# Eighty loads instead of eighty-eight: joining transfers in a two-layer decode kernel that reads its whole cache

## The chip, the cores and the metric

The kernel runs on one NeuronCore of a Trainium2 chip. The time is that of the device, in microseconds, for one execution; less is better. Beside plain runs there is one execution under the hardware profiler, and all rows below are from it.

## The reference, cut to what matters

Two layers, each used twice in turn: attention over a cached window for one new token of 4 sequences, with 32 heads, and a small MLP. The window is the last 1024 positions.

```python
x = x + A(layernorm(x));  x = x + B(layernorm(x));  x = x + A(layernorm(x));  x = x + B(layernorm(x))
def A(x):                       # B=4, D=640, 32 heads of 128, W=1024 cached positions
    q = x @ wq                                  # wq 640 x 4096
    p = softmax(einsum(q, k_cache[-W:]) * Dh**-0.5)
    return einsum(p, v_cache[-W:]) @ wo         # wo 4096 x 640
def B(x):
    return relu(x @ w1) @ w2                    # w1 640 x 1728, w2 1728 x 640
```

All of it is float32. Both rounds use the same caches and weights, and on-chip memory holds about a sixth of them, so nearly everything is read twice from HBM.

## The kernel before, in words

**Records.** For each head the host lays out one record of 9472 columns on 128 partitions (`REC`): columns 0 to 640 are wq (`WQ`), 640 to 4736 the keys (from `K`), 4736 to 8832 the values (from `V`), 8832 to 9472 wo (from `WO`). `VH` is 2048, half of the keys or the values. One column over 128 partitions is 512 bytes, so a record is 4,736 KB and 640 columns are 320 KB. `wm` holds w1 (five blocks of 1728 columns) and w2 (54 tiles of 160).

**Rounds.** `order` gives the heads: 0 to 31 in round one; in round two the five heads still on chip, 27 to 31, come first, then 0 to 26. `store` holds five whole records and 2,176 columns more; `home` says in which of its five slots a head lies. A small tile `kept` holds the end of head 26, and `ring` takes MLP weights and some pieces.

**Loads.** All loads stand in one list, `items`, in a fixed order, and all are issued by SyncE. `pump` issues the next one as soon as the columns that it overwrites are no longer in `live`; `done` and `free` take columns out of `live` after the last instruction that reads them. `pump` is called while the program is built, so on the chip this becomes a wait of the load for that instruction. `group` loads five records in three transfers (`FIVE`), `LAST_FIVE` in four. `ending` cuts the last three heads of a round (a, b and c) into keys and values. In round one `ending` also loads, last of all, the wo of the last six heads (`late`), 26 to 31. The list `places` fills the places that come free at the start of round two.

**Eight semaphores.** Transfers signal their landing on eight semaphores in turn (`DMAHW0` to `DMAHW7`). A transfer that is issued while the one eight places before it is still under way waits until that one has landed. So the moment of such an issue tells when the transfer eight places before it landed.

**Compute.** For each head `query` projects q, `scores` multiplies with the keys in two halves, `softmax` and `weights` run on VectorE and ScalarE, `values` multiplies with the values in two halves, `picks` and `output_T` gather the head's output, and `project` multiplies with wo into `acc`. In the loop the order on TensorE is: scores of head n+1, values of head n, query of head n+2, output and projection of head n. `center` and `deviation` are the layer norm, `mlp` the MLP, `busy` fills TensorE with matmuls that nobody reads.

**Parking.** At the end of round one the MLP needs room, so `park` copies 2560 columns of head 31 from `store` to PSUM, and `unpark` copies them back, into head 27's slot, at the start of round two.

Every instruction is issued through one helper, so nearly all rows carry its line, L102.

Of the kernel before, what the change touches and what calls it, by code (L numbers as in the profile page):

```python
# [39 lines left out]
B, D, H, DH, W, FF = 4, 640, 32, 128, 1024, 1728  # L40
# [6 lines left out]
WQ, K, V, WO = 0, D, D + 4 * W, D + 8 * W  # L47
REC = 2 * D + 8 * W
HALF = REC // 2
VH = 2 * W  # L50

NS = 5
# [7 lines left out]
KEPT = WO - 4 * 512  # L60
FIRST = K + 3 * 512
# [12 lines left out]
IN_RING = [(2176, 4736, "spare", 0), (4736, 6272, "ring", 0), (6272, 8832, "ring", 1536)]  # L74

CUTS = [*range(0, K, DH), *range(K, WO, 512), *range(WO, REC + 1, FD)]
W1_SLOT = [[0, 1], [2, 3], [4]]
W2_SLOT = [22, 20, 8, 4]
LATE = 6


FIVE = [REC + 6272, 2 * REC - 3072, 2 * REC - 3200]
LAST_FIVE = [REC + 4736, 2 * REC - 4736, REC, REC]
THREE = [REC + HALF, REC + HALF]
GROUPS = [{h: FIVE for h in range(0, 25, 5)}, {6: THREE, 9: FIVE, 14: FIVE, 19: LAST_FIVE}]


class InOrder:
# [21 lines left out]
def decode_kernel(ctx: ExitStack, tc: tile.TileContext, xf, rec, wm, out):  # L110
    nc = tc.nc
    pe, dve, act, pool, sp = (InOrder(tc, e) for e in (nc.tensor, nc.vector, nc.scalar, nc.gpsimd, nc.sync))
# [23 lines left out]
    store = sb.tile([P, FIRST + NS * REC], F32, name="store")  # L136
    kept = sb.tile([P, REC - KEPT], F32, name="kept")
# [39 lines left out]
    LAST = H - NS  # L177


    def home(h, r):  # L180

        if r:
            return FIRST + (h if h >= LAST else h - 6 + LAST) % NS * REC
        return (0 if h < NS else FIRST) + h % NS * REC

    items = []

    at = {("rec", 1, LAST - 1): [(KEPT, REC, "kept", 0)], ("rec", 1, 0): [(0, FIRST, "store", 0)]}
    live = []
    spare = home(H - 1, 0)  # L190
    buffers = {"store": store, "ring": ring, "kept": kept}

    def load(src, lo, hi, buf, col, parts):
        items.append((src[:, lo:hi], buf, col, hi - lo, parts))

    def place(buf, col):
        return ("store", spare + FROM + col) if buf == "spare" else (buf, col)
# [1 line left out]
    def weight(r, lo, hi, buf, col):  # L199
        buf, col = place(buf, col)  # L200
        load(wm, lo, hi, buf, col, [(("w", r), lo, hi, col)])


    def run(r, lo, hi, buf, col):
        parts = [(("rec", r, h), max(lo - h * REC, 0), min(hi - h * REC, REC), col + max(h * REC - lo, 0))
                 for h in range(lo // REC, (hi - 1) // REC + 1)]
        load(rec, lo, hi, buf, col, parts)

    def piece(r, h, lo, hi, buf="store", col=None):
        run(r, h * REC + lo, h * REC + hi, buf, home(h, r) + lo if col is None else col)  # L210


    def group(r, h, sizes):
        lo = 0
        for size in sizes:
            run(r, h * REC + lo, h * REC + lo + size, "store", home(h, r) + lo)
            lo += size

    def ending(r, hs, late):
        a, b, c = hs[-3:]  # L220
        end = WO if late else REC
        for h, lo, hi in ((a, 0, V), (b, 0, V), (a, V, end), (c, 0, V), (b, V, end), (c, V, WO if late else KEPT)):
            piece(r, h, lo, hi)
        if late:
            for h in hs[-1:] + hs[-LATE:-1]:
                if h == LAST - 1:
                    piece(r, h, WO, REC, "kept", WO - KEPT)
                else:
                    piece(r, h, WO, REC)


    hs = order[0]
    for h in hs[:-3]:
        if h in GROUPS[0]:
            group(0, h, GROUPS[0][h])
        if h >= 25:
            piece(0, h, 0, KEPT if h == LAST - 1 else WO if h >= H - LATE else REC)
        if h == LAST - 1:
            piece(0, h, KEPT, WO, "kept", 0)
    ending(0, hs, True)  # L240
    for lo, hi, buf, col in MLP_RING:
        weight(0, lo, hi, buf, col)


    hs = order[1]
# [4 lines left out]
    for lo, hi, buf, col in IN_RING:  # L250
        piece(1, new[0], lo, hi, *place(buf, col))
    places = [("store", old[i] + lo, old[j] + hi) for i, lo, j, hi in (
        (0, 0, 0, K), (0, K + 1024, 0, K + VH), (0, K + VH + 1536, 0, V), (1, 0, 1, K), (1, K, 1, K + VH), (1, K + VH, 1, V),
        (0, V, 0, WO), (2, 0, 2, V), (1, V, 1, REC), (3, 0, 3, V), (2, V, 2, REC), (3, V, 4, FROM))]
    places += [("store", 0, FIRST), ("store", old[4] + FROM, old[4] + REC), ("ring", 0, RING)]
    cuts = [h * REC + x for h in new[1:6] for x in CUTS]
    c, end = new[1] * REC, new[6] * REC
    for buf, lo, hi in places:
        if lo == old[1]:
            piece(1, new[0], WO, REC, buf, lo)  # L260
        elif c < end:
            cut = max(x for x in cuts if x <= min(end, c + hi - lo))
            run(1, c, cut, buf, lo)
            c = cut
    assert c == end
    for h in new[6:-3]:
        if h in GROUPS[1]:
            group(1, h, GROUPS[1][h])
        if not any(g <= h < g + sum(z) // REC for g, z in GROUPS[1].items()):
            piece(1, h, 0, REC)  # L270
    ending(1, hs, False)
    for ks in W1_SLOT:
        weight(1, ks[0] * FF, (ks[-1] + 1) * FF, "store", home(LAST + 1, 0) + ks[0] * FF)
    n = 0
# [4 lines left out]
    def pump():  # L279

        while items:
            src, buf, col, n, parts = items[0]
            if any(b == buf and x < col + n and col < y for b, x, y in live):
                return
            sp.dma_start(buffers[buf][:, col:col + n], src)
            live.append((buf, col, col + n))
            for key, lo, hi, c in parts:
                at.setdefault(key, []).append((lo, hi, buf, c))
            items.pop(0)

    def pieces(key):
# [9 lines left out]
    def done(key, lo, hi):  # L301

        if key[0] == "rec" and key[1] == 0 and key[2] >= LAST:
            return
        if key == ("rec", 0, 0):
            lo = max(lo, FIRST)
        for x, y, buf, col in pieces(key):
            free(buf, col + max(lo, x) - x, col + min(hi, y) - x)
        pump()
# [12 lines left out]
    def park(i):  # L322
        a = spare + FROM
        to, lo, hi = ((misc, 0, 512), (t_ps, 512, 1024), (sc_ps[1], 1024, 2048), (o_ps, 2048, 2560))[i]
        act.copy(to, store[:, a + lo:a + hi])
        free("store", a + lo, a + hi)
        pump()

    def unpark(i):
        b = home(LAST, 0)  # L330
        a = b + (K, K + 512, K + VH, K + VH + 512, K + VH + 1024)[i]
        copy = dve.tensor_copy if i in (0, 2) else act.copy
        copy(store[:, a:a + 512], (sc_ps[1][:, :512], sc_ps[1][:, 512:], o_ps, misc, t_ps)[i])
        live.append(("store", a, a + 512))
        if i == 2:
            dve.memset(o_ps, 0.0)
        if i == 4:
            c = spare
            at["rec", 1, H - 1] = [(0, FROM, "store", c), (FROM, V, "store", a - 512), (V, V + 1024, "store", b + K),
                                   (V + 1024, V + 1536, "store", b + K + VH), (V + 1536, REC, "store", c + V + 1536)]  # L340


    h_ps, warm = sc_ps[0][:, :512], sc_ps[0][:, 512:]
# [152 lines left out]


    pump()
    pe.matmul(acc[:, :FD], to_blocks, x_rows, start=True, stop=False, skip_group_check=True)
    for r in range(2):  # L500
        hs = order[r]
        late = LATE if r == 0 else 2
# [6 lines left out]
        if r:  # L509
            unpark(2)  # L510
            unpark(3)
        weights(0, ((0, 1), (1, 2)))
        for n, h in enumerate(hs[:-2]):
            i = n - (H - late)
# [5 lines left out]
            end = n == H - 3  # L520
# [82 lines left out]
```

## Time and profile before

| | |
|---|---|
| time, median of 3 runs | 711.78 us (711.56 to 711.82) |
| the profiled execution's own time | 712.25 us |
| its span, first to last instruction | 710.5 us |
| bytes read from HBM | 301.34 MB, 424 GB/s over the span |
| busy share of TensorE, VectorE, ScalarE | 72%, 41%, 14% |
| mean granted TensorE clock | 0.803 |

A span has 1.7 us around it in this execution (712.25 less 710.5). The rows are of the span, in microseconds from its start.

### The profile page before, as it was taken

To read this page: it belongs to the slowest core of one execution; us is meant where nothing else is said; L and a number is where in the kernel's file an instruction comes from. 1 tells how busy PE (TensorE), PEld (TensorE's weight loads), DVE (VectorE), ACT (ScalarE), POOL (GpSimd) and SP (SyncE) were. 2 spreads that over 40 slices of the span, in tenths; PEclk is the share of its full clock that TensorE was granted. 3 is DMA by queue.
4 is the path that set the end of the run, shared out by engine and by line. 5 is a ranking of instruction groups with operands and counts; after the bars stand their busy time and mean duration, and the time that the engine had idled before them with its cause. 6 is when DMAs were issued, how large, how long until landed. Compare 5 with 4: busy or idle time off the path is not lost.

```text
span 710.5 us, 8480 instructions
## 1 busy us (share of the span) xinstructions
PE 513.0 (72%) x3722; PEld 214.0 (30%) x3722; DVE 293.3 (41%) x518; ACT 99.7 (14%) x210; POOL 1.1 (0%) x9
## 2 busy tenths in 40 slices
PE   0777586677584578869888999656584678686986
PEld 0332232232331223333323443222241232332322
DVE  3242353243342343435531775525162243453651
ACT  0110110011010110111120422101010011011110
POOL 0000000000000000000000000000000000000000
PEclk9977787677778776877999999968597677777989
DMA  9999999999999999999999999999999999999996
GB/s 398 439 416 447 425 435 443 414 439 450 418 435 441 424 437 421 423 439 423 430 398 403 412 426 433 445 435 437 431 435 426 438 436 430 432 432 416 433 425 281
DMA packets 12596, 301.96 MB, mean 425 GB/s; under 512 B 1408, under 2 KB 1552, under 8 KB 4624
## 3 DMA queue, kind: packets, MB, share of 16 engines
q1 hardware_dynamic: 12528, 301.42, 98.9%
q8 instruction: 29, 0.48, 0.2%
q14 instruction: 7, 0.06, 0.0%
q10 hardware_dynamic: 32, 0.01, 0.0%
HBM read 301.34 MB, written 0.08 MB: 424 GB/s over the span
## 4 chain that ended last, share of the span: by engine, by line
DMA 72%; PE 23%; DVE 4%; issue 1%; ACT 1%; ACTq 0%; SPq 0%; DVEq 0%
DMA store<-rec 65%; PE sc_ps L102 9%; PE o_ps L102 6%; DMA store<-wm 4%; PE acc L102 3%; PE misc L102 3%; DMA ring<-wm 2%; DVE scratch L102 2%; PE t_ps L102 1%; DVE o_ps L102 1%; ACT oTs L102 1%; DVE small L102 0%; DVE sc_ps L102 0%; ACT sc_ps L102 0%; ACTq L102 0%
## 5 line engine op out<-in xcount | busy, mean ns | idle before, releaser
L102 PE MATMUL sc_ps<-store,qT 128*32 128x512 f32 x1024 | 194.5, 849 | 35.7 <-DMA store<-rec 34.3
L102 PE MATMUL misc<-xT,store 128*128 128x4 f32 x620 | 95.6, 281 | 109.8 <-DMA store<-rec 109.8
L102 DVE TENSOR_REDUCE small<-sc_ps 128x1 f32<-128x1024 f32 x64 | 78.4, 1224 | 181.3 <-PE sc_ps L102 181.2
L102 PE MATMUL o_ps<-store,scratch 128*16 128x512 f32 x960 | 149.5, 701 | 1.7 <-DMA store<-rec 1.4
L102 PEld LDWEIGHTS misc<-xT,store 128*128 128x128 f32 x620 | 90.2, 227 | 166.6 <-DMA store<-rec 119.4
L102 ACT ACTIVATE sc_ps<-sc_ps,small 128x1024 f32<-128x1024 f32 x64 | 69.8, 1091 | 322.6 <-DVE small L102 322.6
L102 DVE STREAM_TRANSPOSE sc_ps<-sc_ps 128x1024 f32<-128x1024 f32 (+1 forms) x70 | 80.8, 1155 | 0.1
L102 PEld LDWEIGHTS sc_ps<-store,qT 128*32 128x32 f32 x1024 | 41.5, 139 | 112.4 <-issue 60.7
L102 PEld LDWEIGHTS o_ps<-store,scratch 128*16 128x16 f32 x960 | 33.8, 117 | 117.4 <-issue 107.8
L102 DVE TENSOR_TENSOR o_ps<-o_ps,of_block 128x512 f32<-128x512 f32 x62 | 43.3, 699 | 50.6 <-PE o_ps L102 50.6
L102 DVE TENSOR_TENSOR qT<-misc,rows 128x4 f32<-128x4 f32 x61 | 9.5, 155 | 112.9 <-PE misc L102 112.9
L102 PE MATMUL acc<-store,oTs 128*4 128x160 f32 x488 | 34.1, 363 | 17.0 <-ACT oTs L102 17.0
L102 DVE TENSOR_REDUCE scratch<-o_ps 128x128 f32<-128x512 f32 x62 | 42.9, 691 | 2.1
L102 ACT COPY oTs<-t_ps 128x4 f32<-128x4 f32 x59 | 9.6, 163 | 207.4 <-PE t_ps L102 207.4
L102 PE MATMUL t_ps<-rows,scratch 128*128 128x4 f32 x118 | 25.8, 289 | 11.3 <-DVE scratch L102 10.3
L102 PEld LDWEIGHTS t_ps<-rows,scratch 128*128 128x128 f32 x118 | 21.9, 231 | 17.4 <-DVE scratch L102 13.1
L102 DVE SCALAR_TENSOR_TENSOR scratch<-sc_ps,small,of_batch 128x128 f32<-128x128 f32 (+1 forms) x70 | 23.7, 339 | 3.5 <-PE o_ps L102 0.9
L102 PE MATMUL acc<-kept,small 128*1 128x328 f32 (+2 forms) x54 | 17.7, 433 | 0.0
L102 PEld LDWEIGHTS acc<-store,oTs 128*4 128x4 f32 x488 | 7.1, 84 | 22.5 <-ACT oTs L102 22.1
L102 ACT ACTIVATION_READ_ACCUMULATOR sc_ps<-sc_ps,small 128x1 f32 x64 | 12.3, 193 | 0.0
L102 DVE RECIPROCAL small<-small 128x1 f32<-128x1 f32 x64 | 9.8, 153 | 2.3 <-ACT sc_ps L102 2.3
L102 PE MATMUL acc<-store,scratch 128*4 128x160 f32 x146 | 6.1, 299 | 3.3 <-DMA store<-wm 3.2
(83 smaller groups left out, 99.8 us busy)
## 6 DMA issues: line engine op xcount, KB each, us to landing
store<-rec SPq DMA_DIRECT2D x14, 7872.0 KB, 27.3
store<-rec SPq DMA_DIRECT2D x7, 7936.0 KB, 29.9
store<-rec SPq DMA_DIRECT2D x4, 7104.0 KB, 30.8
store<-rec SPq DMA_DIRECT2D x11, 2368.0 KB, 36.5
store<-rec SPq DMA_DIRECT2D x3, 4736.0 KB, 25.7
store<-rec SPq DMA_DIRECT2D x2, 4416.0 KB, 29.1
store<-rec SPq DMA_DIRECT2D x3, 2048.0 KB, 40.7
store<-rec SPq DMA_DIRECT2D x1, 4160.0 KB, 21.6
```

The source lines that it names most:

```text
L102: r = build(*args, **kwargs)
```

## The change

Nothing is computed otherwise; only transfers are cut otherwise.

- Late wo: head 26's goes to `kept` first, then those of heads 27 to 31 go with one transfer of 128 x 5 x 640 into the five slots (`late_outputs`). Before, six transfers in the order 31, 26, 27, 28, 29, 30. The host reorders these five in the record, because slots lie in another order than heads.
- Five pairs joined: head 25 with the start of head 26 (9472 + 6784 columns); the last group of five in three transfers instead of four (`FIVE` for `LAST_FIVE`); w1 of round two in two transfers instead of three; at the start of round two 1024 + 512 columns as 1536, and 2048 + 2048 as 4096. For the last two `unpark` puts its five blocks side by side instead of in two places.
- The values of head 31 in round one in two transfers of 2048 columns instead of one of 4096.

```diff
-W1_SLOT = [[0, 1], [2, 3], [4]]
+W1_SLOT = [[0, 1, 2], [3, 4]]
...
-LAST_FIVE = [REC + 4736, 2 * REC - 4736, REC, REC]
...
-GROUPS = [{h: FIVE for h in range(0, 25, 5)}, {6: THREE, 9: FIVE, 14: FIVE, 19: LAST_FIVE}]
+GROUPS = [{h: FIVE for h in range(0, 25, 5)}, {6: THREE, 9: FIVE, 14: FIVE, 19: FIVE}]
...
+    def late_outputs():
+
+        slots = [(home(h, 0) + WO, home(h, 0) + REC) for h in range(LAST, H)]
+        src = rec.rearrange("p (h c) -> p h c", c=REC)[:, LAST:, WO:]
+        dst = store[:, FIRST:].rearrange("p (h c) -> p h c", c=REC)[:, :, WO:]
+        items.append((src, dst, [("store", a, b) for a, b in slots],
+                      [(("rec", 0, LAST + i), WO, REC, a) for i, (a, _) in enumerate(slots)]))
...
-        for h, lo, hi in ((a, 0, V), (b, 0, V), (a, V, end), (c, 0, V), (b, V, end), (c, V, WO if late else KEPT)):
+        for h, lo, hi in ((a, 0, V), (b, 0, V), (a, V, end), (c, 0, V), (b, V, end)):
             piece(r, h, lo, hi)
+        for lo, hi in ((V, V + VH), (V + VH, WO)) if late else ((V, KEPT),):
+            piece(r, c, lo, hi)
         if late:
-            for h in hs[-1:] + hs[-LATE:-1]:
-                if h == LAST - 1:
-                    piece(r, h, WO, REC, "kept", WO - KEPT)
-                else:
-                    piece(r, h, WO, REC)
+            piece(r, LAST - 1, WO, REC, "kept", WO - KEPT)
+            late_outputs()
...
-        if h >= 25:
-            piece(0, h, 0, KEPT if h == LAST - 1 else WO if h >= H - LATE else REC)
-        if h == LAST - 1:
-            piece(0, h, KEPT, WO, "kept", 0)
+        if h == LAST - 2:
+            run(0, h * REC, h * REC + REC + KEPT, "store", home(h, 0))
+            piece(0, LAST - 1, KEPT, WO, "kept", 0)
+        elif h >= LAST:
+            piece(0, h, 0, WO)
...
-        (0, 0, 0, K), (0, K + 1024, 0, K + VH), (0, K + VH + 1536, 0, V), (1, 0, 1, K), (1, K, 1, K + VH), (1, K + VH, 1, V),
+        (0, 0, 0, K), (0, K + VH + 512, 0, V), (1, 0, 1, K), (1, K, 1, V),
...
-        a = b + (K, K + 512, K + VH, K + VH + 512, K + VH + 1024)[i]
+        a = b + K + 512 * i
```

On SyncE, at the end of round one, the list of loads before has the last values (4096 columns), six pieces of wo and the first MLP weights (`ring`):

```order
26 L102 DMA store<-rec 128x4096 [waits DMAHW2_49,PE_49]
27 L102 DMA store<-rec 128x640 [waits DMAHW3_49]
28 L102 DMA kept<-rec 128x640 [waits DMAHW4_49]
29 L102 DMA store<-rec 128x640 [waits DMAHW5_49]
30 L102 DMA store<-rec 128x640 [waits DMAHW6_49]
31 L102 DMA store<-rec 128x640 [waits DMAHW7_49]
32 L102 DMA store<-rec 128x640 [waits DMAHW0_49]
33 L102 DMA ring<-wm 128x1728 [waits DMAHW1_49,DVE_49,Pool_49]
34 L102 DMA ring<-wm 128x1728 [waits DMAHW2_49]
```

On SyncE, at the same place of the changed kernel:

```order
25 L101 DMA store<-rec 128x2048 [waits DMAHW1_49,PE_49]
26 L101 DMA store<-rec 128x2048 [waits DMAHW2_49]
27 L101 DMA kept<-rec 128x640 [waits DMAHW3_49]
28 L101 DMA store<-rec 128x5x640 [waits DMAHW4_49]
29 L101 DMA ring<-wm 128x1728 [waits DMAHW5_49,DVE_49,Pool_49]
30 L101 DMA ring<-wm 128x1728 [waits DMAHW6_49]
```

The last values come in two halves, five pieces have become one of 128x5x640, and `ring` loads follow four places earlier.

On TensorE, at the end of round one, before: the last values (`sc_ps`, from `store` and `scratch`), the transposes of the last two outputs (from `rows`), and the projections of the six late heads (`acc`, from `oTs`):

```order
284 L102 MATMUL o_ps<-rows,scratch 128x4 [waits DVE_49]
285 L102 MATMUL acc<-kept,oTs 4x160 [waits DMAHW4_49]
286 L102 MATMUL acc<-kept,oTs 4x160 x3
287 L102 MATMUL acc<-store,oTs 4x160 [waits DMAHW5_49]
288 L102 MATMUL acc<-store,oTs 4x160 x3
289 L102 MATMUL acc<-store,oTs 4x160 [waits DMAHW6_49]
290 L102 MATMUL acc<-store,oTs 4x160 x3
291 L102 MATMUL sc_ps_73<-rows,scratch 128x4 [waits DVE_49]
292 L102 MATMUL acc<-store,oTs 4x160 [waits DMAHW7_49,Activation_49]
```

On TensorE, the same place of the changed kernel:

```order
279 L101 MATMUL sc_ps_73<-store,scratch 16x512 [waits DMAHW1_49,DVE_49,Activation_49]
280 L101 MATMUL sc_ps_73<-store,scratch 16x512 x3
281 L101 MATMUL sc_ps_73<-store,scratch 16x512 [waits DMAHW2_49,DVE_49]
282 L101 MATMUL sc_ps_73<-store,scratch 16x512 x3
283 L101 MATMUL o_ps<-rows,scratch 128x4 [waits DVE_49]
284 L101 MATMUL acc<-kept,oTs 4x160 [waits DMAHW3_49]
285 L101 MATMUL acc<-kept,oTs 4x160 x3
286 L101 MATMUL acc<-store,oTs 4x160 [waits DMAHW4_49]
287 L101 MATMUL acc<-store,oTs 4x160 x7
288 L101 MATMUL sc_ps_73<-rows,scratch 128x4 [waits DVE_49]
```

The two halves of the last values now wait for a transfer each, and the projections after `kept` wait once, for the joined transfer, where they waited for one small transfer per head.

On SyncE, at the start of round two, before, the loads that fill the places of heads 27 and 28:

```order
47 L102 DMA store<-rec 128x640 [waits PE_49]
48 L102 DMA store<-rec 128x1024 [waits PE_49]
49 L102 DMA store<-rec 128x512 [waits PE_49]
50 L102 DMA store<-rec 128x640 [waits PE_49]
51 L102 DMA store<-rec 128x2048 [waits PE_49]
52 L102 DMA store<-rec 128x2048 [waits DMAHW4_49,PE_49]
53 L102 DMA store<-rec 128x3840 [waits DMAHW5_49,PE_49]
```

On SyncE, there in the changed kernel:

```order
43 L101 DMA store<-rec 128x640 [waits PE_49]
44 L101 DMA store<-rec 128x1536 [waits PE_49]
45 L101 DMA store<-rec 128x640 [waits PE_49]
46 L101 DMA store<-rec 128x4096 [waits PE_49]
47 L101 DMA store<-rec 128x3840 [waits PE_49]
```

Each joined load stands where its second half stood, and waits for the later of the two releases.

## Rows read from the trace of the kernel before

**Rows 1.** The page: packets of all queues.

```profile
DMA packets 12596, 301.96 MB, mean 425 GB/s; under 512 B 1408, under 2 KB 1552, under 8 KB 4624
```

**Rows 2.** The page: share of the last-ending chain by engine.

```profile
DMA 72%; PE 23%; DVE 4%; issue 1%; ACT 1%; ACTq 0%; SPq 0%; DVEq 0%
```

**Rows 3.** Windows: stretch, busy of PE, PEld, DVE, ACT, POOL, clock, DMA share, GB/s.

```profile
460.00:560.00 100.00, 58.76 (x416) 24.73 (x416) 34.51 (x56) 10.94 (x24) 0.00 (x0) 0.74 1.00 434
364.00:402.00 38.00, 32.90 (x342) 13.79 (x334) 14.32 (x40) 7.83 (x15) 0.00 (x0) 1.00 0.99 395
```

**Rows 4.** Timeline of SyncE, four issues: start, duration, load.

```profile
350.04 0.33 SPq L102 DMA_DIRECT2D store<-rec  x1
354.94 0.33 SPq L102 DMA_DIRECT2D ring<-wm  x1
359.75 0.33 SPq L102 DMA_DIRECT2D ring<-wm  x1
360.53 0.33 SPq L102 DMA_DIRECT2D ring<-wm  x1
```

**Rows 5.** DMA issues: count, KB each, median us from issue to landing.

```profile
store<-rec SPq DMA_DIRECT2D x11, 2368.0 KB, 36.5
...
store<-rec SPq DMA_DIRECT2D x3, 1024.0 KB, 8.1
...
out<-scratch SPq DMA_DIRECT2D x1, 80.0 KB, 1.6
```

**Rows 6.** Windows at the end of round one, two stretches, columns as in rows 3.

```profile
360.50:363.90 3.40, 3.40 (x26) 1.01 (x22) 0.89 (x2) 0.73 (x3) 0.00 (x0) 0.50 1.05 430
363.90:367.30 3.40, 3.37 (x56) 1.79 (x52) 1.63 (x7) 1.82 (x3) 0.00 (x0) 1.00 1.02 410
```

**Rows 7.** Timeline, end of round one, PE, DVE and SyncE.

```profile
359.87 3.06 PE L102 MATMUL sc_ps<-store,scratch 128*16 128x512 f32 x16 [2.45 <-DVE scratch L102]
...
363.38 0.68 PE L102 MATMUL acc<-kept,oTs 128*4 128x160 f32 x8
...
363.87 0.74 PE L102 MATMUL acc<-store,oTs 128*4 128x160 f32 x16
...
364.85 1.05 PE L102 MATMUL acc<-store,oTs 128*4 128x160 f32 x24
...
365.97 0.33 DVE L102 TENSOR_REDUCE small<-acc 128x1 f32<-128x160 f32 x1 [0.68 <-PE acc L102]
...
368.18 3.13 SPq L102 DMA_DIRECT2D ring<-wm  x3
...
374.35 0.91 PE L102 MATMUL sc_ps<-ring,xT 128*4 128x432 f32 x8 [0.45 <-DMA ring<-wm]
```

**Rows 8.** Timeline of SyncE, the second of each joined pair in round two.

```profile
392.17 0.33 SPq L102 DMA_DIRECT2D store<-rec  x1
395.64 0.33 SPq L102 DMA_DIRECT2D store<-rec  x1
```

**Rows 9.** Timeline of PE: the query of head 27, round one.

```profile
317.60 2.30 PE L102 MATMUL misc<-xT,store 128*128 128x4 f32 x10 [3.99 <-DMA store<-rec]
```

**Rows 10.** Timeline of PE, round two: third load of a group of five lands.

```profile
599.26 0.96 PE L102 MATMUL sc_ps<-store,qT 128*32 128x512 f32 x3 [2.87 <-DMA store<-rec]
...
605.96 0.48 PE L102 MATMUL acc<-store,oTs 128*4 128x160 f32 x8 [0.31 <-ACT oTs L102]
```

**Rows 11.** Timeline of PE, the last heads and the last MLP.

```profile
656.22 1.28 PE L102 MATMUL misc<-xT,store 128*128 128x4 f32 x10 [3.60 <-DMA store<-rec]
658.14 0.72 PE L102 MATMUL acc<-store,oTs 128*4 128x160 f32 x8 [0.30 <-ACT oTs L102]
673.77 1.90 PE L102 MATMUL o_ps<-store,scratch 128*16 128x512 f32 x16
678.60 1.28 PE L102 MATMUL misc<-xT,store 128*128 128x4 f32 x10 [0.75 <-DMA store<-rec]
704.90 2.79 PE L102 MATMUL acc<-store,scratch 128*4 128x160 f32 x68 [1.88 <-DMA store<-wm]
```

More of the change, by code (lines that the diff above doesn't have):

```diff
@@ L193, in load @@
     def load(src, lo, hi, buf, col, parts):
-        items.append((src[:, lo:hi], buf, col, hi - lo, parts))
+        items.append((src[:, lo:hi], buffers[buf][:, col:col + hi - lo], [(buf, col, col + hi - lo)], parts))
+    def late_outputs():
[4 more added lines that the diff above has]
+                      [(("rec", 0, LAST + i), WO, REC, a) for i, (a, _) in enumerate(slots)]))
     def place(buf, col):
@@ L281, in pump @@
         while items:
-            src, buf, col, n, parts = items[0]
-            if any(b == buf and x < col + n and col < y for b, x, y in live):
+            src, dst, spans, parts = items[0]
+            if any(b == buf and x < hi and lo < y for b, x, y in live for buf, lo, hi in spans):
                 return
-            sp.dma_start(buffers[buf][:, col:col + n], src)
-            live.append((buf, col, col + n))
+            sp.dma_start(dst, src)
+            live.extend(spans)
             for key, lo, hi, c in parts:
-                at.setdefault(key, []).append((lo, hi, buf, c))
+                at.setdefault(key, []).append((lo, hi, spans[0][0], c))
             items.pop(0)
@@ L339, in unpark @@
             at["rec", 1, H - 1] = [(0, FROM, "store", c), (FROM, V, "store", a - 512), (V, V + 1024, "store", b + K),
-                                   (V + 1024, V + 1536, "store", b + K + VH), (V + 1536, REC, "store", c + V + 1536)]
+                                   (V + 1024, V + 1536, "store", b + K + 1024), (V + 1536, REC, "store", c + V + 1536)]
     h_ps, warm = sc_ps[0][:, :512], sc_ps[0][:, 512:]
@@ L583 @@
     rec[:, :, V:WO] = v.reshape(B, H, W // 32, 32, DH).transpose(1, 0, 3, 2, 4).reshape(H, P, -1)
-    rec[:, :, WO:] = np.asarray(A_wo).reshape(H, DH, D)
+    wo = np.asarray(A_wo).reshape(H, DH, D)
+    rec[:, :, WO:] = wo
+    rec[H - NS:, :, WO:] = wo[[next(h for h in range(H - NS, H) if h % NS == i) for i in range(NS)]]
     w2 = np.asarray(B_w2)
```

## The prediction

> **What bounds the kernel now.** I read the page first. Its chain of work that ended last gives 72% of the span to DMA and 23% to TensorE [rows 2]. So the kernel is bound by the stream of loads: 302 MB have to come in [rows 1], and compute matters only where it lets that stream run empty, or where work is left after the last byte.
>
> Then the windows, to see how full the stream is. In a stretch of large loads 434 GB/s move at a DMA share of 1.00; from 364 to 402 us, around the first MLP and the start of round two, the share is 0.99 but only 395 GB/s move [rows 3]. That is 38 us x (1 - 395/434) = 3.4 us of lost movement, the one place in the middle of the run where the stream is not at its best. There the places are few, and each load waits for TensorE to free one.
>
> Last, the end: TensorE waits 1.88 us for w2, then works 2.79 us [rows 11], and the output of 80 KB needs 1.6 us [rows 5]. The change touches none of these three.
>
> **What a transfer costs in a full stream.** Before, four issues at the end of round one wait for the landing of the transfer eight places ahead, so their times are landing times [rows 4]. What landed are head 31's queries and keys (at 350.04), two transfers of 2,048 KB (354.94 and 359.75) and one of 320 KB (360.53). The two took 4.90 and 4.81 us, the small one 0.78. The slope is (4.855 - 0.78) / 1,728 KB = 2.36 us per 1,000 KB, and at this slope 320 KB are 0.755 us. What is left for a transfer as such is 0.78 - 0.755 = 0.025 us. With either of the two large ones alone it is 0.01 or 0.03, and since issue times carry some hundredths of error I let it reach from 0.01 to 0.05.
>
> The Trainium skill ("DMA: Bandwidth & Descriptors", section "Anatomy of one DMA — SWDGE (gpsimd) path") gives a fixed part of about 2.0 us per DMA beside bytes over 436 GB/s, fitted on loads that GpSimd issues. By it each transfer saved would be worth up to 2 us. The 0.78 us for a whole 320 KB transfer speak against that here: the fixed part lies beside the transfers in front.
>
> **The change, term by term.**
>
> *Transfers saved.* Nine are taken out (four of the late wo, five by pairs) and one is added, so eight: 8 x 0.025 = 0.2 us, and 0.1 to 0.4 by the bounds. The late five remain 640 runs of 2,560 bytes, and no row shows a transfer of several runs per partition: its four may save nothing, which leaves 0.1 of the sum; nothing in it moves more bytes, so I see no loss. I take them as the others, -0.2.
>
> The same page says in "Why a DMA increments its semaphore by 16 and not by 1" that one descriptor moves one contiguous run. By that the joined five keep their descriptors, and the sum would be -0.1 instead of -0.2.
>
> *Late wo as one.* The first small piece lands at 360.53 [rows 4], and five more at 0.78 us each end at 364.4. In the changed order the piece for `kept` lands first, near 360.5, and the five together at about 364.4. Before, the projections of heads 27 and 28 (16 instructions) ran at 363.87, ahead of that; the last three heads (24 instructions) started at 364.85, and `center` at 365.97 [rows 7]. Afterwards all 40 and the transpose between them come after 364.4: 0.74 + 1.05 us and 0.3 for the transpose (363.87 + 0.74 to 364.85, rounded up), so `center` starts at 366.5, 0.5 us late.
>
> That is at the clock of 363.90 to 367.30, granted 1.00 (2.4 GHz), before which TensorE was busy for all of 3.40 us at 0.50 (1.2 GHz) [rows 6]. In the changed kernel it stands idle before 364.4. If it is granted 0.50 there, eight instructions take 0.68 us [rows 7], the 40 take 3.4 and the transpose 0.6, and `center` is at 368.4, 2.4 us late.
>
> Who waits for that? Behind `center` are the first MLP products, and they free `ring`: the next load was issued at 368.18, and TensorE waited for it until 374.35, 6.2 us [rows 7]. Alone, that load of 864 KB would need 1.4 us (the output's 1.6 less 0.2 for its 80 KB) [rows 5] and 2.0 to move, 3.4 us. So it was issued 2.7 us before the stream came to it. A delay of 0.5 is hidden in these 2.7, and one of 2.4 just so; if the first products run at 0.50 too, add the 0.9 us that eight of them took [rows 7], and 0.6 us come through. I take 0 and keep 0 to 0.6.
>
> *Last values in halves.* Their 16 instructions ran from 359.87 for 3.06 us [rows 7], after the whole 4,096 columns. With halves, eight can run 2.4 us earlier, and the rest ends 1.5 us earlier. But the projections wait for 364.4 anyway, so nothing comes of it: 0.
>
> *Pairs at the start of round two.* Each joined load waits for the second release, 392.17 and 395.64 [rows 8]. The second is the tighter. Before, a load of 1,024 KB was issued at 395.64 and landed 8.1 us later, at 403.8 (8.1 is the median of three [rows 5]; one of the others stands a transfer before it, the third in a deep queue near the end). A load of 2,048 KB issued then needs 1.4 + 4.8 = 6.2 us and could be in at 401.9. So 1.9 us of cover are left: 0. Without that cover the price is what the first half's earlier issue bought, about 0.9 us.
>
> *Heads 25 and 26 together.* Head 25 now lands with the 3,392 KB of head 26, 8.0 us later at the slope above. TensorE waited 3.99 us before the query of head 27 [rows 9], so it may be some 4 us late there. The loads that follow wait for places that it frees, but eleven loads of 2,368 KB have a median of 36.5 us from issue to landing [rows 5], so 4 us are covered: 0.
>
> *The last group in three.* Head 22's last columns now come with head 23, at 656.2 instead of 11 us earlier. The same pattern stands one group before: from the third landing at 599.26 to the end of the projection behind it, 605.96 + 0.48, are 7.2 us [rows 10]. So the projection at 658.14 [rows 11] ends at 663.4 and not 658.9, 4.5 us late. Of that, 2.9 us disappear before head 26's query (673.77 + 1.90 to 678.60), where matmuls that nobody reads stand, and the remaining 1.6 are less than the 1.88 us for which TensorE waits before the last w2 [rows 11]: 0. The loads behind it are issued later, but deep in the queue. w1 in two transfers lands in full when it did, and I count no wait for it.
>
> **Sum.** -0.2 us and zeros: 712.25 - 0.2 = 712.05 us for an execution like the profiled one, which is 0.47 above the median, so **711.6 us** against 711.78. Under 0.2% (1.4 us), which is about what a measurement of this kernel can tell from no change, this is no change.
>
> **The rivals.**
>
> *The stream runs empty (slower).* Place: the first `ring` reload. Late wo arrives all at once, TensorE is granted 0.50, and from a delay of 2.7 us on every microsecond is lost. For it: 0.50 was granted just before [rows 6], and this stretch already loses 3.4 us. With 0.6 through, and the pairs' 0.9 lost because everything there starts late, it is 711.78 - 0.2 + 1.5 = 713.1 us. Chance 14%.
>
> *The tail is uncovered (slower).* The last group's 4.5 us meet a clock of 0.50 for another head. 16 instructions of values took 3.06 us at 359.87, mostly at 0.50, and 1.90 at 673.77 [rows 7, 11]; with as many of scores that is 2.3 us per head. It decides from 4.8 us of delay on (2.9 + 1.9), and one head gives 4.5 + 2.3 - 4.8 = +2.0: 713.6 us. Against it: the 7.2 us are from a pattern that began after 2.87 us of idle time as well. Chance 6%.
>
> *A transfer costs more (faster).* From 364 to 402, 3.4 us lost over some twenty transfers is 0.17 us each, seven times what the full stream shows. If that were the price of each of the eight, 8 x 0.17 = 1.4 us: 710.4 us. Against it: only two of the eight lie there. Chance 13%.
>
> *The fixed part counts in full.* If a transfer's 1.4 us beside its bytes stood alone in the stream, 8 x 1.4 = 11 us: 700.6. The 0.78 us deny it; under 1%.
>
> By the page named first it would be 8 x 2.0 = 16 us, 695.8 us.
>
> **Numbers.** The forecast, 711.0 to 712.2, has 66%. The range reaches into the rivals on both sides and leaves out their far halves: 710.3 to 713.0. Faster by over 0.2% (below 710.4): 9 of the 13 points of the dear transfer, 1 of the fixed part, 3 for what I don't see, 13%. Slower (above 713.2): half of the empty stream's 14 and 5 of the tail's 6, 12%. Same: 75%.
>
> **What the changed profile would show.** Packets under 512 B fall from 1408 [rows 1] to 1280, by sixteen for each transfer. 460 to 560 stays at 434 GB/s, 364 to 402 near 395; below 385 there, the stream ran empty and the first rival holds. The late projections start together near 364.4, `center` between 366.5 and 368.4. Near 656 TensorE starts the work of two heads, is some 4 us late at the next projection and in time for the last w2; if its wait there is gone, the tail is uncovered. I am wrong if the last w2 lands more than 1.4 us earlier or later than before.

## The result, and the profile after

The changed kernel takes **714.94 us** (median of 6 runs, 713.62 to 718.45) where the kernel before takes 711.80 (6 runs, 711.30 to 712.24). The ratio is 1.0047, with a 95% interval of 1.0033 to 1.0062, so it is 3.3 us slower (2.3 to 4.4). The forecast was 711.6 us in a range up to 713.0, and no change; it was wrong. The profiled execution took 713.62 us with a span of 711.9, against 712.25 and 710.5 before. It is the fastest of the six, so its profile shows 1.4 of the 3.1 us that lie between the medians.

First the page: packets, and the chain that ended last.

```profile
DMA packets 11956, 301.96 MB, mean 424 GB/s; under 512 B 1280, under 2 KB 1424, under 8 KB 4240
...
DMA 63%; PE 29%; DVE 5%; ACT 1%; another core or an unknown queue 1%; issue 1%; SPq 0%; ACTq 0%; DVEq 0%
```

The small packets fell by 128, sixteen for each of the eight transfers [rows 1]; the same bytes come in. Then the windows of the two stretches of [rows 3], with the same columns:

```profile
364.00:402.00 38.00, 32.18 (x316) 13.77 (x316) 12.52 (x38) 6.91 (x12) 0.00 (x0) 0.96 0.96 370
460.00:560.00 100.00, 63.69 (x428) 26.47 (x420) 36.47 (x59) 12.14 (x26) 0.00 (x0) 0.72 1.00 432
```

The stretch of large loads is as before. The stretch of the first MLP and the start of round two moves 370 GB/s, not 395: 38 x (395 - 370)/434 = 2.2 us of movement lost. Where it begins, in the timeline of the changed kernel:

```profile
364.48 1.25 PE L101 MATMUL acc<-store,oTs 128*4 128x160 f32 x16 [2.87 <-DMA store<-rec]
...
366.18 1.68 PE L101 MATMUL acc<-store,oTs 128*4 128x160 f32 x24
...
367.94 0.33 DVE L101 TENSOR_REDUCE small<-acc 128x1 f32<-128x160 f32 x1 [1.32 <-PE acc L101]
...
370.15 0.33 SPq L101 DMA_DIRECT2D ring<-wm  x1
...
374.47 0.99 PE L101 MATMUL sc_ps<-ring,xT 128*4 128x432 f32 x8
...
378.17 0.53 PE L101 MATMUL sc_ps<-ring,xT 128*4 128x432 f32 x1 [2.16 <-DMA ring<-wm]
```

TensorE waits 2.87 us for the joined late wo and then has all 40 projections to do. The first row of `center` is at 367.94 (365.97 before), the first `ring` reload is issued at 370.15 (368.18) [rows 7]. The matmuls on that reload run at 374.47, almost when they did (374.35). The delay comes through one load later: what ran at 376.38 before, in the first row here, now runs at 378.17. The other rows are windows, of before, again before, of the changed kernel, twice:

```profile
376.38 0.53 PE L102 MATMUL sc_ps<-ring,xT 128*4 128x432 f32 x1 [0.58 <-DMA ring<-wm]
```

```profile
368.00:372.00 4.00, 3.49 (x21) 1.18 (x20) 0.18 (x1) 0.26 (x1) 0.00 (x0) 1.00 0.93 361
364.00:404.00 40.00, 34.90 (x358) 14.27 (x350) 15.33 (x41) 7.83 (x15) 0.00 (x0) 1.00 1.00 397
```

```profile
368.00:372.00 4.00, 3.96 (x30) 1.46 (x29) 1.25 (x6) 0.26 (x1) 0.00 (x0) 1.00 0.68 237
364.00:404.00 40.00, 33.93 (x338) 14.69 (x342) 13.92 (x39) 7.56 (x14) 0.00 (x0) 0.96 0.96 372
```

From 368 to 372 the DMA share is 0.68 and 237 GB/s move: the stream runs out of loads. It did so a little before, too, at 361 GB/s.

The chain that ended last goes over that second load, with nothing between its landing and its use. Its pieces, first before, then in the changed kernel (start, duration):

```profile
369.74 6.59 DMA ring<-wm
...
376.38 0.44 PE sc_ps L102
...
392.18 1.23 DVE small L102
```

```profile
371.71 6.41 DMA ring<-wm
...
378.17 0.44 PE sc_ps L101
...
394.10 1.23 DVE small L101
```

So this load had no cover before the change either. The delay of 1.97 us goes on along the chain: the first softmax of round two (`small`) starts 1.92 us later. And the clock:

```profile
360.80:364.21 3.41, 0.81 (x14) 0.41 (x10) 1.39 (x2) 0.75 (x2) 0.00 (x0) 1.00 1.03 423
364.21:367.63 3.42, 3.15 (x42) 1.70 (x43) 0.09 (x1) 1.32 (x2) 0.00 (x0) 0.50 1.03 427
```

TensorE was busy for 0.81 us of the first stretch, and in the second, which holds the projections, it was granted 0.50 (1.2 GHz). Before, that level lay on the last values, and the projections had 1.00 [rows 6].

The end, in the changed kernel, and its counterpart before:

```profile
705.01 4.04 PE L101 MATMUL acc<-store,scratch 128*4 128x160 f32 x112
...
708.60 0.11 PEld L101 LDWEIGHTS acc<-store,scratch 128*4 128x4 f32 x8 [0.21 <-DMA store<-wm]
```

```profile
707.23 0.11 PEld L102 LDWEIGHTS acc<-store,scratch 128*4 128x4 f32 x8 [0.34 <-DMA store<-wm]
```

The wait of 1.88 us before the last w2 [rows 11] is gone. The last eight weight loads of TensorE still wait 0.21 us for theirs, 1.37 us later than before, and the span is 1.4 us longer. So in this execution the end moved with the loads, and the work behind the last group comes out even with them: from 657.42 on the chain that ended last has no load in it any more.

It doesn't stay even in every kernel. Before, and in e8 (the changed kernel once more), the last stretch of 0.1 us in which loads moved bytes, and the issue of the output:

```profile
706.80:706.90 0.10, 0.10 (x12) 0.10 (x3) 0.00 (x0) 0.00 (x0) 0.00 (x0) 1.00 0.06 26
708.11 0.35 SPq L102 DMA_DIRECT2D out<-scratch  x1
```

```profile
709.70:709.80 0.10, 0.10 (x12) 0.08 (x6) 0.00 (x0) 0.00 (x0) 0.00 (x0) 1.00 0.07 26
711.64 0.35 SPq L101 DMA_DIRECT2D out<-scratch  x1
```

Between them lie 1.21 us before and 1.84 in e8. In the profiles of e11, e12, e14 and e15 it is 1.98 to 2.17, in all others 1.21 to 1.37. In these five the end is set by work, and an estimate from these figures is that 0.5 to 0.9 us are lost there. All five have the last group in three; so have six others in which nothing is lost at the end.

### The profile page after: what moved, and what is told of

Same layout as the page of the kernel before. It is cut to its first block, busy times and chain, and to the rows that moved or that the text cites. A ratio compares the mean times of both kernels' runs of the same rounds, so it can differ in the third digit from the quotient of the medians.

```text
span 711.9 us, 8466 instructions
## 1 busy us (share of the span) xinstructions
PE 509.3 (72%) x3722; PEld 215.1 (30%) x3722; DVE 292.9 (41%) x518; ACT 99.6 (14%) x210; POOL 1.1 (0%) x9
## 4 chain that ended last, share of the span: by engine, by line
DMA 63%; PE 29%; DVE 5%; ACT 1%; another core or an unknown queue 1%; issue 1%; SPq 0%; ACTq 0%; DVEq 0%
DMA store<-rec 61%; PE sc_ps L101 12%; PE o_ps L101 8%; PE acc L101 5%; PE misc L101 3%; DVE scratch L101 2%; DMA ring<-wm 2%; DVE o_ps L101 2%; PE t_ps L101 2%; ACT oTs L101 1%; DVE small L101 0%; ACT sc_ps L101 0%; DVE sc_ps L101 0%; ACTq L101 0%
## 5 line engine op out<-in xcount | busy, mean ns | idle before, releaser
L101 PE MATMUL sc_ps<-store,qT 128*32 128x512 f32 x1024 | 192.5, 837 | 37.0 <-DMA store<-rec 35.6
L101 PE MATMUL misc<-xT,store 128*128 128x4 f32 x620 | 97.3, 284 | 111.0 <-DMA store<-rec 111.0
L101 PE MATMUL o_ps<-store,scratch 128*16 128x512 f32 x960 | 148.0, 690 | 3.1 <-DVE small L101 1.4
L101 PEld LDWEIGHTS misc<-xT,store 128*128 128x128 f32 x620 | 91.9, 230 | 168.5 <-DMA store<-rec 118.8
```

Of the source, the lines that this page charges most:

```text
L101: r = build(*args, **kwargs)
```

## The experiments

All ratios are to the kernel before, run beside it on the same chip (medians of 711.80 to 712.61 us). They aren't the quotients of the medians: e13, at 0.9994, has a median of 712.50 where before has 712.40. The columns "reload" (issue of the first `ring` reload) and GB/s of two stretches are of the one profiled execution of each.

| run | ratio, 95% interval | reload, us | 368 to 372 | 364 to 404 |
|---|---|---|---|---|
| before | 1 | 368.18 | 361 | 397 |
| changed | 1.0047 (1.0033 to 1.0062) | 370.15 | 237 | 372 |
| e8, changed, again | 1.0038 (1.0023 to 1.0052) | 371.24 | 196 | 358 |
| e1, last group in four again | 1.0062 (1.0048 to 1.0077) | 371.17 | 190 | 360 |
| e14, places apart | 1.0034 (1.0021 to 1.0047) | 371.22 | 200 | 362 |
| e3, late wo apart | 1.0018 (1.0006 to 1.0031) | 368.86 | 336 | 392 |
| e13, both apart | 0.9994 (0.9984 to 1.0003) | 368.04 | 369 | 397 |
| e4, late wo alone | 1.0020 (1.0010 to 1.0030) | 369.13 | 298 | 392 |
| e10, pairs alone | 1.0021 (1.0010 to 1.0032) | 368.54 | 347 | 385 |
| e9, halves alone | 0.9996 (0.9988 to 1.0005) | 367.76 | 375 | 405 |
| e2, last group alone | 0.9998 (0.9988 to 1.0007) | 367.70 | 377 | 401 |
| e7, changed, filled | 1.0011 (1.0003 to 1.0020) | 369.14 | 311 | 381 |
| e16, the same again | 1.0016 (1.0006 to 1.0025) | 369.03 | 309 | 383 |
| e15, filled, places apart | 1.0012 (0.9999 to 1.0026) | 369.45 | 286 | 384 |
| e12, more filled, places apart | 1.0031 (1.0015 to 1.0047) | 369.15 | 302 | 394 |
| e5, 1 us of delay | 0.9998 (0.9989 to 1.0007) | 368.11 | 366 | 404 |
| e6, 2 us of delay | 1.0024 (1.0009 to 1.0038) | 371.30 | 216 | 372 |
| e11, no loss expected, filled | 1.0009 (1.0000 to 1.0018) | 368.55 | 357 | 398 |

The edits by which the kernels differ:

```diff
 # late wo apart (e3, e13, e11): the six transfers of before
-            piece(r, LAST - 1, WO, REC, "kept", WO - KEPT)
-            late_outputs()
+            for h in hs[-1:] + hs[-LATE:-1]:
...
 # places apart (e14, e13, e15, e12, e11): the places and unpark of before
-        (0, 0, 0, K), (0, K + VH + 512, 0, V), (1, 0, 1, K), (1, K, 1, V),
+        (0, 0, 0, K), (0, K + 1024, 0, K + VH), (0, K + VH + 1536, 0, V), (1, 0, 1, K), (1, K, 1, K + VH), (1, K + VH, 1, V),
...
 # filled (e7, e16, e15, e12 with 6; e11 with 1)
             project(r, hs[H - late + i], i, False)
+            for _ in range(6 if late > 2 and not i else 0):
+                busy()
...
 # more filled (e12, e11)
-        values(r, hs[-1], 1)
+        values(r, hs[-1], 1, (0 if r else 3, 0))
...
 # delay (e5 with 3, e6 with 6; only in round one's MLP)
-        dve.tensor_reduce(sums, x, op=OP.add, axis=AX.X)
+        for _ in range(1 + again):
+            dve.tensor_reduce(sums, x, op=OP.add, axis=AX.X)
```

**First: which part.** The theory was that two parts cost: the late wo, and the last group. In e1 the changed kernel has `LAST_FIVE` again; in e2 the kernel before has `FIVE` there and nothing else; e3 has the late wo apart; e4 has the kernel before with the late wo joined and nothing else.

> The changed kernel with one part undone: the last group of five again in four transfers. Two mechanisms are held to share the loss of 3.1 us: late wo as one transfer (the first MLP reload is issued 2 us later, 1.4 us in the profiled run) and the last group in three (TensorE is late to the end, and how late hangs on its granted clock, so times scatter over 5 us). Then this kernel is at 713.2 us (711.8 + 1.4) and its runs lie within 1 us of one another. If late wo makes all of the loss: 714.9 and still scattered. If the last group makes all of it: 711.6.

> The kernel before with one part of the change alone: the last group of five in three transfers. Two mechanisms: about 713.5 us in the median, 711.8 at the least, with runs scattered over several us, and in the profile no wait of TensorE before the last w2 products. If late wo makes all of the loss: 711.8 with a spread of half a microsecond. If the last group makes all of it: 714.9.

> The changed kernel with one part undone: late wo again in six transfers in the order of before. Two mechanisms: near 713.5 us, scattered by the tail, and the first reload of ring issued near 368.2 again. If the last group makes all of the loss: 714.9. If late wo makes all of it: 711.6 without scatter.

> The kernel before with one part of the change alone: late wo in two transfers (head 26, then the five as one), last values in one. Two mechanisms: 713.2 us, runs within 1 us, the first reload of ring issued near 370 and the window of 364 to 402 under 390 GB/s. If the last group makes all of the loss: 711.7.

e2 measured 711.81 us and e1 716.80. The last group alone costs nothing that can be told, undoing it gives nothing back, and that half of the theory falls. e4 (713.50) shows that the late wo alone costs 0.20%, 1.4 us. e3 (713.24, reload at 368.86 where 368.2 was expected) shows that something among the rest costs about as much. In e4 the chain stands by itself, at the full clock:

```profile
364.83 0.73 PE L102 MATMUL acc<-store,oTs 128*4 128x160 f32 x16 [1.98 <-DMA store<-rec]
...
365.80 1.05 PE L102 MATMUL acc<-store,oTs 128*4 128x160 f32 x24
...
366.92 0.32 DVE L102 TENSOR_REDUCE small<-acc 128x1 f32<-128x160 f32 x1 [0.69 <-PE acc L102]
...
369.13 0.33 SPq L102 DMA_DIRECT2D ring<-wm  x1
```

`center` is 0.95 us late, the reload 0.95 us, and 368 to 372 moves 298 GB/s: 4 x (361 - 298)/434 = 0.6 us are lost there alone. The joined transfer itself moves no slower: 360 to 364 us moves 429 GB/s before and in e4, and 427 in the changed kernel.

**Second: the cover, and the clock.** e5 and e6 change no transfer. They only delay the layer norm ahead of the reload. e7 fills TensorE's wait for the joined late wo, and e8 is the changed kernel again.

> The kernel before, with the sum in the layer norm ahead of the first MLP taken four times instead of once: three more instructions of 0.33 us on VectorE, so all behind it starts 1.0 us later and the first ring reload is issued near 369.2 instead of 368.18. No transfer is changed. Theory of the prediction (that load has 2.7 us of cover): 711.9 us, nothing lost, and 368 to 372 us moves 361 GB/s as before. Theory 'no cover' (at 368.18 the queue has already all but run out, so each microsecond later is a microsecond without bytes): about 712.8 us, and 368 to 372 us falls to about 300 GB/s, as in the run with late wo joined alone, whose reload was 0.95 us late.

> The same with six more instructions, 2.0 us. Theory of the prediction: 711.9 us, since 2.0 is still less than 2.7. Theory 'no cover': reload near 370.2, 713.7 us, and 368 to 372 us near 237 GB/s, as in the changed kernel, whose reload was at 370.15. If this one costs clearly less than the changed kernel, the late reload isn't all of that kernel's loss.

> The changed kernel, with six matmuls that nobody reads (328 columns, about 0.36 us each at the full clock) on TensorE between the projection of head 26 and that of head 27, where it stands idle for 2.9 us waiting for the joined late wo. Theory 'the idle time lowers the clock': the granted clock stays 1.00 through the projections and the layer norm, 40 projections take 2.0 us instead of 3.4, the first ring reload is issued near 369.1 instead of 370.15, and the time falls by about 1.2 us against the changed kernel in the same call. Rival, 'the clock falls there by chance or for another reason': the reload stays near 370.15 and the time near the changed kernel's.

> The changed kernel once more, as it is, to stand beside the other three on the same chip: its first six runs spread from 713.6 to 718.5, and the one with its last group in four again gave 716.8, which no theory of mine explains. 714.9 if the first result holds. If it gives 716 to 717 here, then the last group in four costs nothing in that run either, and the difference of the two lies in where the low clock falls.

By its times e5 speaks against 'no cover' as it was put: 712.78 us at a ratio of 0.9998 is at most 0.5 us slower, where 0.9 was expected. Its profile tells why, for one execution. The low clock lay at 351.26 to 354.67 (first fence), earlier than in the one of before, `center` started at 364.83 in spite of an unchanged program up to there (second), and the reload went out at 368.11:

```profile
351.26:354.67 3.41, 3.29 (x16) 0.60 (x16) 1.05 (x4) 0.00 (x0) 0.00 (x0) 0.50 1.00 428
360.50:363.90 3.40, 3.23 (x52) 1.44 (x48) 2.17 (x4) 1.57 (x5) 0.00 (x0) 1.00 1.05 427
```

```profile
364.83 1.40 DVE L102 TENSOR_REDUCE small<-acc 128x1 f32<-128x160 f32 x4 [0.96 <-PE acc L102]
...
368.11 3.13 SPq L102 DMA_DIRECT2D ring<-wm  x3
```

e2, which has the program of before up to this place, shows the same without the delay:

```profile
364.81 0.33 DVE L102 TENSOR_REDUCE small<-acc 128x1 f32<-128x160 f32 x1 [1.03 <-PE acc L102]
...
366.74 0.91 PE L102 MATMUL sc_ps<-ring,xT 128*4 128x432 f32 x8 [0.52 <-DMA ring<-wm]
...
367.70 3.54 SPq L102 DMA_DIRECT2D ring<-wm  x3
```

There TensorE waits 0.52 us for the first MLP weights. In e5 the same products start at 366.99, so of 1.0 us of delay 0.25 reaches them and 0.41 the reload: the rest is hidden behind the weights ahead of the reload. That tells nothing of the reload's own cover. How often the low clock lies there isn't known.

e6 (714.10 us) tells more: 0.6 to 2.7 us were lost. Its rows:

```profile
366.38 2.48 DVE L102 TENSOR_REDUCE small<-acc 128x1 f32<-128x160 f32 x7 [0.68 <-PE acc L102]
371.30 0.33 SPq L102 DMA_DIRECT2D ring<-wm  x1
```

```profile
368.00:372.00 4.00, 3.08 (x18) 1.23 (x22) 1.60 (x7) 0.23 (x1) 0.00 (x0) 0.75 0.52 216
364.00:404.00 40.00, 33.55 (x338) 14.14 (x334) 16.70 (x47) 8.10 (x15) 0.00 (x0) 0.96 0.95 372
```

The reload came 3.1 us late, not 2.0: `center` starts 0.4 late ahead of the delay already, and behind it the clock falls (0.75 in the first window). A cover of 2.7 us would let 0.4 of that through; the whole interval lies above, though not by much. In the profile this kernel moves as little from 364 to 404 as the changed one, and it has all 88 transfers. So a late layer norm and reload alone cost 1.7 us. Whether that is all of the changed kernel's loss isn't told, since the intervals overlap.

e8 gave 715.69 us, e7 713.56, and the two intervals don't meet. In e8 the low clock lasts through the projections and the layer norm (first fence), in e7 none falls there (second and third):

```profile
360.10:363.51 3.41, 1.34 (x18) 0.41 (x10) 1.39 (x2) 0.75 (x2) 0.00 (x0) 1.00 1.06 431
363.51:370.34 6.83, 5.95 (x55) 2.77 (x56) 1.21 (x6) 1.45 (x2) 0.00 (x0) 0.50 0.89 369
```

```profile
361.55 3.47 PE L101 MATMUL acc<-kept,small 128*1 128x328 f32 x12
364.61 0.96 PE L101 MATMUL acc<-store,oTs 128*4 128x160 f32 x16
```

```profile
364.00:368.00 4.00, 3.96 (x52) 1.87 (x51) 0.91 (x5) 1.45 (x2) 0.00 (x0) 1.00 1.01 421
```

The six unread matmuls of the program are twelve instructions, 3.47 us. They put the reload at 369.14, where it was expected, and take 0.27% off, 1.9 us, where 1.2 was expected; in e8 the reload came at 371.24 and not at 370.15. e8's 715.69, 0.38% above before, bears out the first result.

**Third: the other parts alone, and a better kernel.** e9 is the kernel before with the halves only, e10 with the two pairs at the start of round two only; e11 and e12 as in the diff.

> The kernel before, with nothing changed but the values of head 31 in round one, loaded in two halves. By the prediction it is worth nothing, 711.9 us. By the theory 'what counts is when the first ring reload is issued, and idle time before it lowers the clock': TensorE is through with the values 1.5 us earlier, stands idle for the late wo, and where the lower clock falls on the projections and the layer norm the reload is issued near 368.9 (as in the run with all but the late wo), some 0.5 us are lost, 712.4; where it falls elsewhere the reload is near 367.6 and the time 711.6. So between 711.6 and 712.4, with the reload telling which.

> The kernel before, with nothing changed but the two joined loads at the start of round two (1024 + 512 columns, 2048 + 2048). By the prediction 1.9 us of cover, nothing lost: 711.9 us. By the theory that this stretch has no cover either, each joined load waits for the second release and the queue is short of bytes for that time: 396 to 400 us falls below the 375 GB/s of before, and up to 0.9 us are lost, 712.6. In the four runs with them so far this stretch moved 350 to 390 GB/s, which tells neither.

> Of the changed kernel only what cost nothing: last group in three, w1 in two, head 25 with 26, the last values in halves. The late wo in six transfers and the loads at the start of round two apart, as before. And four matmuls that nobody reads in the waits of TensorE ahead of the late projections (three between the two halves of the last values, one behind head 26's projection). If the reload's issue sets the time, and the clock stays at 1.00 there, the reload comes near 367.5, ahead of the 368.18 of before, and the time is 0.5 us under the kernel before in the same call. If the reload's issue has nothing to do with it: the same as before.

> The changed kernel with the idle time ahead of the joined late wo filled (nine matmuls that nobody reads) and the two pairs at the start of round two apart. What is left of the change that could cost anything is the late wo as one transfer. Reload near 369.1, 0.9 us later than before, as in the run with nothing else changed; of that run's 1.5 us lost, some 1 us here: 713.0 where before is at 712.0. If it is no slower than before, the pairs were the rest of the loss; if it stays at 713.5 like the filled one, they cost nothing.

e9 (711.94 us): nothing lost, nothing gained that can be told. e10 (713.59): the pairs alone cost 0.21%, 1.5 us (0.7 to 2.3). The stretch in which they lie, before and in e10:

```profile
394.00:402.00 8.00, 7.60 (x68) 2.93 (x64) 6.95 (x14) 3.34 (x7) 0.00 (x0) 1.00 1.00 398
```

```profile
394.00:402.00 8.00, 7.61 (x64) 2.81 (x60) 7.08 (x14) 3.48 (x7) 0.00 (x0) 1.00 0.98 370
```

8 x (398 - 370)/434 = 0.5 us are lost there. The sign that was named didn't come: 396 to 400 moves 379 GB/s, not less than the 375 of before. But the longer stretch, 394 to 402, bears it out over all profiles: 370 to 394 GB/s in the seven that have the pairs joined (381 in the mean), 387 to 417 in the eleven that don't (406). By that 8 x 25/434 = 0.5 us are lost in this stretch, an estimate. From 364 to 404 it is 40 x (397 - 385)/434 = 1.1 us; some of this comes ahead of the pairs, with a reload 0.36 us later in that one execution, and so isn't theirs. e11 (712.69) missed: the reload was at 368.55, not 367.5, and it is no better than before. In its profile some 0.8 us are lost at the end, where the output is issued 1.98 us after the last bytes of the loads. e12 (714.09) missed too, by 1.1 us upward, with its reload where it was expected; it loses as much at the end (2.16 us), but so does e15 below, at 713.19.

**Fourth: is it a sum?**

> The changed kernel without the two parts that cost about 1.5 us each when they stood alone: the late wo in six transfers again, the loads at the start of round two apart. No fills. Theory 'the loss lies in those two and adds up': no slower than the kernel before in the same call, 711.7 us where that has 712.0. If it is slower by 1 us or more, a part that cost nothing alone (last group, w1, head 25 with 26, halves) costs something beside the others.

> The changed kernel with only the loads at the start of round two apart. By the same theory what is left is the late wo: 713.5 us, as in the run with it alone, or up to 714.5 where the low clock falls on the projections. If the pairs were not a cost of their own but came through only with a late reload, this gives 715, as the changed kernel.

> That kernel with the six unread matmuls ahead of the joined late wo, and without the three more between the last values that the run before had. That run gave 714.1 where the filled one with the pairs gave 713.6, against both prices of 1.5 us. If the three more were what cost: 713.0 here. If it is 714 again, the price of the pairs isn't the same beside the late wo, or a run of this size has a scatter of 1 us from the place of the low clock.

> The filled changed kernel once more, on the same chip as the three above. 713.6 us (0.11% above the kernel before) if the first result holds; by the prices of 1.5 us for the pairs and 1.5 us less what the fills give for the late wo it should be near 714.5. The clock theory needs it under the changed kernel's 0.38 to 0.47%.

e13 (712.50 us, ratio 0.9994): without the late wo and the pairs nothing is lost, so the loss lies in these two and in what the rest does beside them. It isn't shown to be faster than before. e14 (714.97): the late wo with the halves costs 0.34%, 1.0 us more than the late wo alone in e4 (the intervals overlap), and its profile has the low clock and the late reload of e8. e15 (713.19) and e16 (713.29): filled, the price of the late wo is 0.12 to 0.16%, with the pairs or without. So beside the late wo the pairs cost 0.04 to 0.13% (e14 against e8 and the changed kernel) or 0.04% (e15 against e16), though 0.21% alone. Each of these differences is uncertain by about 0.2% either way, so whether the two parts add isn't shown. e12's excess over e15 (the three more fills) is within two wide intervals.

## Why the prediction was wrong, step by step

**The step that failed: "So it was issued 2.7 us before the stream came to it."** It took the moment at which TensorE's products start, 374.35, less 3.4 us for a load by itself, and called the rest cover. Three things were wrong with it.

The load by itself was under-sized: issued into a nearly empty queue at 370.15 its products ran at 374.47, 4.3 us, not 3.4. That leaves 6.2 - 4.3 = 1.9 us of cover by this way of counting.

It was the wrong load. The chain goes over the next one, issued at 369.74 because it waits for products behind the same `center`, in at 376.34, and used at once: TensorE waits 0.58 us for it. Its cover was 0, and a later `center` passes through it: 1.97 us later issued, 1.79 later used.

And a wait from issue to use is no cover where the stream itself is short. The first reload was issued 1.97 us later and its products ran 0.12 us later, as if covered; but 237 GB/s instead of 361 moved meanwhile. The row that could have told was to be had: 368 to 372 us of the kernel before at 361 GB/s and a share of 0.93.

A load is in only when its last part is in, so parts of the stream can be without work while it is awaited. The Trainium skill ("DMA: Bandwidth & Descriptors", section "Why a DMA increments its semaphore by 16 and not by 1") says that the engines of a transfer, up to sixteen, finish independently and that only the full count means that all has landed. No view here shows the sixteen apart, so this part of the account is argued and not shown.

What the runs showed in place of the 2.7 us: no cover on the load that the chain goes over, a loss of 1.4 us for a reload 0.95 late (e4), and of 1.7 for one 3.1 late without any joined transfer (e6).

**Late wo as one, the rest of the term.** The chain was right: projections near 364.4 (measured 364.48), `center` between 366.5 and 368.4 by the clock (366.92 in e4 at 1.00, 367.94 and a low clock in the changed kernel). Priced without cover it would have been 0.95 us and up to 3.1 us of a late reload, where 0 was taken and 0.6 kept. Measured alone: 1.4 us.

**Pairs at the start of round two.** "1.9 us of cover are left: 0" was taken from landing times of whole loads too, and e10 measured a loss of 1.5 us. The price named for the case without cover, about 0.9 us, lies in the measured 0.7 to 2.3. That the later issue is the cause is argued from the bytes of 394 to 402 us; no run delays these loads alone.

**Last values in halves.** 0 by themselves (e9), right. Beside the joined late wo they make TensorE's idle time longer (2.87 us in the changed kernel, 1.98 in e4), and the reload is at 371.2 in e8, e1 and e14 and at 370.15 in the changed kernel, against 369.13 in e4, each in one execution. The prediction had the wait and the possible 0.50, but counted the halves at 0 since "the projections wait for 364.4 anyway".

**Heads 25 and 26, the last group, w1.** 0 held for the last group alone (e2) and for all three with the halves (e13). But the working left 0.3 us of the wait before the last w2, and the tail rival's sign, that wait gone, is there in e2 and in the changed kernel. In e8, e11, e12, e14 and e15 the end lies later than the loads by 0.5 to 0.9 us. Undoing the group (e1) gave nothing back all the same; that e1 is above the changed kernel isn't explained. The prediction's own sign of being wrong, the last w2 over 1.4 us later, stayed off by a hair in the profile, at 1.37.

**Transfers saved.** -0.2 us stays unmeasured: e13, with three joined and one cut, is 0.06% faster with an interval that reaches 0.03% slower.

**The rivals.** "The stream runs empty" had the right place, cause and sign (370 GB/s against its mark of 385), at 14%, and was sized at 1.5 us because it too began from a cover of 2.7. Without it, the prediction's own delays at the lower clock, 2.4 us, or 3.3 with slow first products, with 0.9 for the pairs and less the 0.2, would have given 3.1 to 4.0 above 711.8; measured were 2.3 to 4.4. That this agrees so well is in part luck: how much of it is the pairs', and how much the tail's, isn't told. "A transfer costs more" spread the missing 3.4 us over transfers; but with eight transfers fewer it moved still less there, 370 GB/s, so the price isn't one per transfer.

## What to carry to other kernels

A load's cover isn't how long it lies between its issue and its use. Look at the bytes that move just ahead of its landing: where the windows already show less than the full rate, as at 361 of 434 GB/s here, a later issue came through. And follow the chain that ended last: a load that it passes, and that is used as soon as it is in, has no cover. A delay ahead of another wait can still be hidden, as in e5. Joining transfers there makes each place wait for the later release and each reader for the last byte, and in this case saved nothing that could be measured. When a wait on TensorE grows, look also at what the lower clock falls on behind it; twelve unread matmuls in that wait gave back 1.9 us.

## What was not expected of the hardware

The place of the lower clock differs between executions of the same instructions. The changed kernel had it from 364.21 to 367.63 in its first profile and from 363.51 to 370.34 in its second (e8), and the reload was at 370.15 and at 371.24. Before, it lay at 360.50 to 363.90 [rows 6]; in e5, with the same program up to `center`, it lay earlier, and `center` started 1.1 us sooner. That is as much as most parts here cost, so one profile doesn't price such a part; the medians of many runs do.

A load issued into a nearly empty queue took 4.3 us for 864 KB (the changed kernel's first reload), of which 864 KB at 434 GB/s are 2.0. The 2.3 left are far above the 0.025 us that a transfer costs in a full queue. The Trainium skill's fixed part of about 2.0 us ("DMA: Bandwidth & Descriptors", section "Anatomy of one DMA — SWDGE (gpsimd) path") is fitted on DMAs that GpSimd issues. The 2.3 us here, on a load that SyncE issues, are near to it. The prediction had set it aside for a full stream, and the 0.025 us bear that out.
